# Attention and a token/channel mixer on one core: scores of whole 128-key chunks, barred squares cleared after the exponential, and a new written-out order

## The chip, the cores and the metric

One Trainium2 chip, one core. The time is the device time of one execution in microseconds (us); a lower one is better. Most executions of one kernel agree within 0.3%.

## The reference

Block-wise causal attention (blocks of 64 positions, 8 batches, 8 heads, 576 positions, head size 64), and behind it a mixer over positions and over channels:

```python
scores = scale * np.matmul(q, k.transpose(0, 1, 3, 2))        # q, k, v: (8, 8, 576, 64)
mask = block_i >= block_j                                     # block of a position: pos // 64
scores = np.where(mask, scores, -1000000000.0)
attn = np.exp(scores - max);  attn = attn / (sum + 1e-09)
x = (attn @ v) as (8, 576, 512)
h = np.maximum(xt @ w_tok1, 0.0) @ w_tok2                     # xt: x with positions last
u = x + h.transpose(0, 2, 1)
return u + np.maximum(u @ w_ch1, 0.0) @ w_ch2                 # 512 -> 1536 -> 512
```

Within a 128-key chunk that covers the blocks 2J (keys 0 to 63) and 2J+1 (keys 64 to 127), the queries of block 2J may see the first 64 keys and not the last 64. These 64x64 places are the barred squares.

## The kernel before

**A plan.** The kernel does not emit instructions as it computes. Each helper adds operations to a plan (`P.add`): a piece of work of one or several instructions, with the engines that may run it, what it depends on, and the PSUM banks that it takes and gives back. Operations are numbered as they are added. The string `ORDER` then lists the numbers in the order in which they are emitted; the letter behind a number is the engine (T TensorE, A ScalarE, D DVE, P POOL, S SyncE), and small letters name the PSUM banks taken: a to d are `mm`, e to h are `late`, s and t are two pairs of banks that batch 0's scores use. When the last exponential of batch 0 is done, s and t become e to h. Each engine runs its operations in the order of the list and waits where an operand is not there. Loads are issued from POOL's queue, outputs and large transposes from SyncE's.

**Attention.** Each batch has two groups of four heads (`hg`). `load_qk` brings k and q (L419, L437), DVE transposes them into `kT` and `qT` (L442): a head's 64 dimensions lie as two halves (`par` 0 and 1) in 32 partitions, and four heads fill the 128. `score_set` (L569) computes the scores of a group in three sets, `SETS`, each of one bank of 512 columns per head: set 1 (keys of blocks 2 and 3, and a piece of 0), set 2 (blocks 0 and 1), set 0 (blocks 4 to 8). A tuple of `SETS` is (half, key block, first query block, first column, columns, par). `half` says which 64 partitions of the bank the scores go to, so a matmul holds 64 keys as weights, and the two halves of a 128-key chunk are two matmuls. Where a square is barred, a matmul with `bar` (-2.5e8 times 1.0, key block `None`) opens the place, and the exponential makes it zero.

ScalarE writes the exponentials into `e_sb` (L776; for batch 0 L587 and L737, 1024 columns at a time). `ECOL` and `TAIL` say where a chunk's columns lie. `tail` copies the square at `TAIL` for all heads aside (L595) and then clears its last 64 keys (L600), on DVE or POOL. `head_out` multiplies the exponentials, as weights, with the values `v1` (L617) and divides by the sum; `ends_out` does so for the last 64 positions (L670). `load_v` brings the values (L471).

**The mixer.** `token_mix` (L811, L815, L846, L910) and the channel products follow batch by batch; some of these are done in seven products instead of eight (`channel_up_half` L1111, `channel_up_fast` L1235, `channel_down_fast` L1369), whose sums DVE makes and whose banks ScalarE and DVE empty. The outputs leave at L1421 and L1435.

**The start.** `raise_clock` runs 11 matmuls of 512 columns on zeros (L366), and then up to `KEEP` more (L373), which `ORDER` puts between the first operations; those not listed are not emitted.

Of the kernel before, what the change touches and what calls it, by code (L numbers as in the profile page):

```python
# [10 lines left out]
BF16 = mybir.dt.bfloat16  # L11
# [16 lines left out]
class Plan:  # L28
# [69 lines left out]
    16S 0A 11D 10D 13S 9D 21P 1D 2D 43Ta 5D 19P 4D 3D 23P 33P 27P 14A 25P 31P 15D 29P 17A 20D 37P 44Tb 45Tb 46Tb 22D  # L98
    47Ta 36P 48Ta 49Ta 18D 50Ta 51Ta 52Ta 35P 53Ta 24D 54Ta 55Ta 56Ta 125Ts 34P 100Ttbc 179P 126A 28D 57Ta 58Ta 59Ta
    176P 60Ta 61Ta 26D 62Ta 101A 12P 106Ts 63Ta 32D 182P 64Ta 107A 65Ta 104Tt 42P 30D 66Ta 67Ta 105A 68Ta 39P 123Ts  # L100
    102D 103D 69Ta 70Ta 41P 119A 71Ta 157Tt 124A 112Td 40P 113T 116Ta 108Tb 114D 120A 38P 109T 115D 138Ts 158A 181D
    81P 72Td 73Tc 74Tc 121D 75Tc 122D 139A 82P 76Tc 7D 144Tt 110D 111D 84P 135Td 178D 127Tc 145A 161Ts 185P 136D
    117D 137D 140D 131Tb 180D 83P 128T 162A 142Tt 177D 90P 132T 129D 143A 77Td 89P 163Ts 130D 133D 86P 134D 78Td
    164A 118D 141D 159D 200Tdcba 160D 85P 203A 173Te 154Tf 165Tg 202A 91P 174D 166T 155D 156D 201A 184D 92P 205Tbhfc
    204A 183D 169Td 88P 170T 209A 167D 263Ta 168D 208A 175D 150Tc 171D 261Tg 172D 207A 187D 267Td 206A 87P 186D
    146Te 262A 147T 264A 151T 268D 237Tgbfh 152D 339P 6D 148D 269Ta 153D 241A 149D 273Td 189P 240A 270D 281Tc 239A
    274D 265Te 190P 238A 271Ta 8D 282D 275Tb 266A 191P 193Tdhfg 276A 272D 283Te 196A 277Tc 342P 194A 315Ta 278D
    306Tb 197A 188P 294Td 195A 279Tc 284A 192P 318Tf 198D 280D 291Tg 319T 348P 316T 309Tc 317A 310T 257D 93P 320A
    307T 295T 94P 308A 292T 311A 258D 225Teahf 345P 296A 300Tb 227A 95P 285Tc 228A 286T 293D 226A 303Td 287D 229A
    304T 351P 232Tahge 341D 199D 312Tc 230D 233A 305D 313T 234A 231D 288Tf 344D 314A 297Ta 340D 236A 289T 343D 235A  # L110
    210Td 513P 245Tc 290A 211D 213Th 516P 212D 242Te 246D 216Tg 354P 247D 301T 214D 215D 248Td 243D 302A 298T 244D
    355P 217D 219Tc 249D 299A 250D 222Th 220D 254Te 221D 363Tdbaf 255D 256D 251Tc 349D 364A 330Te 352P 252D 365A
    218D 253D 321Td 367A 223D 224D 366A 259D 353P 368Tcghb 420Ta 372A 370A 422Tb 347D 371A 525P 346D 322T 421D 423A
    260D 369A 356Tafgh 323T 359A 357A 350D 424Tb 360A 324D 331T 358A 425D 388Tcadg 361P 514D 430Tb 391A 434Th 332T
    389A 431D 435A 518D 426Td 392A 517D 400Thcbf 390A 515D 428Tg 404A 393P 362D 334Ta 522P 403A 429D 677P 401A 335T
    333D 402A 528P 427D 376Tb 373Tc 394D 527P 96D 395Tdfgh 379Te 526P 377D 396A 374D 336T 375D 397A 519P 378D 380D
    405Tc 398A 680P 381D 382Tb 399A 406D 385Td 407D 432Te 337D 417Tc 383D 386D 433A 530Tafgh 387D 384D 418D 436Td
    419D 531A 440Tb 97D 414Tc 534A 325Te 533A 98D 326T 532A 415D 437A 416D 542Tahgf 99D 441A 438Tc 545A 327T 439D
    544A 444D 463Tgd 543A 445D 448Thb 328D 466A 464Tc 451D 546A 329S 411Ta 408Te 465A 446D 469T 412D 690P 413D 449Tf
    523D 470A 454T 529P 450A 409D 442Ta 410D 452Tc 455A 443D 691P 467Tg 520D 453A 537Taefh 447D 692P 468A 456T 521D  # L120
    538A 473T 689P 524D 539A 471T 679D 540A 683P 596Ta 457D 541A 474D 562Tcefh 597A 678D 458T 566A 681D 594Ta 565A
    459D 564A 460D 476T 563A 595D 461T 477A 569Tchfe 682D 462A 472D 604Ta 847P 571A 478Tdb 475D 686P 572A 605D 602Tg
    535P 481A 600Th 603D 536P 570A 598Ta 567P 482Tf 601D 607S 568P 553Tc 844P 599D 483A 479Tg 550Th 554D 555D 480A
    488T 551D 484T 552D 606S 489D 486T 485A 556Tc 487D 491T 573A 574Thadg 557D 490D 492A 547Te 558D 577A 493D 497Tbf
    575A 548D 576A 549D 559Tc 578A 688D 701Tedah 498A 685D 579Tg 560D 704A 684D 499T 705A 494D 850P 702A 693P 580D
    585Ta 703A 581D 503T 500D 687D 706Tgdbh 586D 587D 561D 591Te 504D 710A 501Ta 709A 495D 708A 592D 707A 593D 582Tc
    502D 627Tbd 612The 608D 630A 588Tg 583D 496D 505T 859P 615D 858P 633T 584D 506D 507T 857P 634A 589D 590D 860P
    694Tcgab 508D 856P 618T 698A 849D 509T 697A 846D 696A 619D 695A 760Tb 609D 610D 699P 510D 738Tacgh 761A 848D
# [42 lines left out]
    1457D 1392D 1492The 1453D 1393T 1488D 1493A 1489D 1455D 1498T 1394D 1458T 1396S 1460T 1490D 1459D 1472Tca 1468D  # L171
    1465S 1461D 1494T 1464S 1473A 1469D 1476Td 1470D 1478T 1491D 1462T 1479D 1471D 1499D 1482T 1463D 1496Tg 1477D
    1466S 1483D 1502T 1467S 1497D 1484T 1503D 1500T 1507S 1485D 1495D 1480T 1487S 1501D 1474T 1506S 1481D 1504T
    1475D 1486S 1505D 1508S
"""


@with_exitstack
def kernel(
# [340 lines left out]

    BARRED = 2.5e8

# [1057 lines left out]
```

## Time and profile before

| | |
|---|---|
| time, median of 3 runs | 284.84 us (284.22, 284.84, 285.99) |
| profiled execution, first to last instruction | 284.7 us |
| instructions | 9438, of which 4038 matmuls and as many weight loads |
| busy: TensorE matmul / weight load | 275.8 us (97%) / 197.6 us (69%) |
| busy: DVE / ScalarE / POOL | 240.3 (84%) / 180.4 (63%) / 71.7 (25%) |
| granted TensorE clock | full in every slice |
| DMA | 31.79 MB, 112 GB/s in the mean |

How to read it: "busy" is the time in which an engine ran at least one instruction, and an average over stages with different limits. PE is TensorE's matmuls, PEld its weight loads. In a group's row stand line, engine, operation, output<-inputs, shape and count, then busy us, the mean ns of one, and the idle time ahead of it with what ended it. The chain of work that ended last is followed back from the last instruction. "issue" there is time in which the engine waited for nothing that the profile shows. A matmul's record ends later than its last column enters; the distance of starts tells the pace. The span of the profiled execution is what the sums of the prediction are made against; no separate time of that execution was taken.

### The profile page before, as it was taken

How to read it: one execution, taken by the hardware profiler on the slowest of the kernel's cores; microseconds unless marked ns; L12 is line 12 of the kernel's file. 1: busy time of each engine (PE TensorE's matmuls, PEld its weight loads, DVE VectorE, ACT ScalarE, POOL GpSimd, SP SyncE). 2: the span in 40 equal slices, each digit the busy share in tenths (PEclk: the TensorE clock that was granted, in tenths of full speed). 3: DMA queues.
4: the chain of work that ended last, by engine and by line, in shares of the span. 5: the costliest groups of instructions: out<-in, count | busy, mean ns of one | idle time of the engine just before them, and what ended most of it. 6: DMA issues, size and time to landing. Idle time of an engine off the chain costs nothing.

```text
span 284.7 us, 9438 instructions
## 1 busy us (share of the span) xinstructions
PE 275.8 (97%) x4038; PEld 197.6 (69%) x4038; DVE 240.3 (84%) x519; ACT 180.4 (63%) x325; POOL 71.7 (25%) x120
## 2 busy tenths in 40 slices
PE   7998999999999899999999999999999999999994
PEld 3667656556878676987777658744488876468883
DVE  3589569799999799999998997997998987598893
ACT  3798685778888358996879785136546653764000
POOL 8975635170641062060341220000000000000000
PEclk9999999999999999999999999999999999999999
DMA  8999999969989495898199587130033403000246
GB/s 160 166 174 202 190 205 203 137 94 134 144 120 119 71 84 87 225 135 122 11 169 102 87 106 132 49 119 18 2 74 98 126 7 131 12 2 0 104 127 212
DMA packets 64776, 31.79 MB, mean 112 GB/s; under 512 B 53088, under 2 KB 55904, under 8 KB 64736
## 3 DMA queue, kind: packets, MB, share of 16 engines
q0 software_dynamic: 45040, 17.64, 53.1%
q1 hardware_dynamic: 19696, 13.57, 19.6%
q8 instruction: 31, 0.51, 0.7%
q14 instruction: 9, 0.07, 0.1%
HBM read 35.85 MB, written 9.44 MB: 159 GB/s over the span
## 4 chain that ended last, share of the span: by engine, by line
PE 92%; DVE 2%; ACT 2%; DMA 1%; issue 1%; SPq 0%; DVEq 0%
PE late L1369 14%; PE mm L1369 11%; PE late L1235 7%; PE mm L1111 7%; PE late L1111 6%; PE mm L569 6%; PE mm L1235 6%; PE mm L617 4%; PE mm L811 3%; PE mm L910 3%; PE mm L1038 3%; PE late L569 2%; PE late L617 2%; PE late L811 2%; PE mm L1460 2%; PE late L1460 2%
## 5 line engine op out<-in xcount | busy, mean ns | idle before, releaser
L776 ACT ACTIVATE e_sb<-late 128x512 bf16<-128x512 f32 x89 | 50.5, 609 | 10.4 <-PE late L569 9.1
L776 ACT ACTIVATE e_sb<-mm 128x512 bf16<-128x512 f32 x79 | 45.1, 609 | 9.9 <-PE late L569 6.6
L471 POOL DMA_DIRECT2D vals<-in_v_dram x45 | 37.2, 844 | 26.7 <-PE late L617 15.9
L442 DVE STREAM_TRANSPOSE qk_sb<-qk_sb 128x288 int32<-128x288 int32 (+2 forms) x57 | 36.2, 694 | 4.6 <-ACT qk_sb L395 3.5
L1369 PEld LDWEIGHTS <-sums 128*128 128x128 bf16 x288 | 27.6, 98 | 5.6 <-issue 1.8
L1369 PEld LDWEIGHTS <-gT 128*128 128x128 bf16 x288 | 27.8, 98 | 4.6
L569 PEld LDWEIGHTS <-qk_sb 32*64 32x64 bf16 x1280 | 19.9, 104 | 13.1 <-issue 8.8
L569 PE MATMUL mm<-qk_sb 32*64 32x64 bf16 (+7 forms) x546 | 27.8, 291 | 0.0
L569 PE MATMUL late<-qk_sb 32*64 32x512 bf16 (+7 forms) x594 | 27.1, 291 | 0.0
L617 PEld LDWEIGHTS <-e_sb 128*128 128x128 bf16 x640 | 23.8, 97 | 4.1 <-issue 0.9
L1111 PEld LDWEIGHTS <-ws_sb 128*128 128x128 bf16 x192 | 17.8, 98 | 3.4 <-issue 1.3
L797 ACT ACTIVATE gT<-mm 128x512 bf16<-128x512 f32 x25 | 14.7, 601 | 7.8 <-PE mm L1111 3.0
L617 PE MATMUL mm<-vals,e_sb 128*128 128x65 bf16 x430 | 19.0, 193 | 0.0
L643 DVE TENSOR_TENSOR x_sb<-mm,rinv 128x256 bf16<-128x256 f32 x43 | 17.9, 421 | 1.1
L1111 PEld LDWEIGHTS <-wc_sb 128*128 128x128 bf16 x144 | 15.4, 114 | 1.8 <-issue 0.2
L1235 PEld LDWEIGHTS <-ws_sb 128*128 128x128 bf16 x96 | 9.3, 98 | 10.1 <-issue 0.2
L1369 PE MATMUL late<-wd_sb,sums 128*128 128x256 bf16 x108 | 13.6, 272 | 1.2 <-issue 1.2
L1369 PE MATMUL late<-wd_sb,gT 128*128 128x256 bf16 x120 | 14.7, 273 | 0.0
L595 POOL COPY vals<-e_sb 128x256 bf16<-128x256 bf16 x10 | 4.1, 412 | 40.9 <-issue 22.9
L395 ACT COPY mm<-late 128x512 f32<-128x512 f32 x17 | 9.9, 584 | 7.1 <-PE late L1235 5.0
L797 ACT ACTIVATE gT<-late 128x512 bf16<-128x512 f32 x17 | 10.2, 602 | 6.3 <-PE late L1235 3.4
L1235 PE MATMUL late<-e_sb,ws_sb 128*128 128x512 bf16 x44 | 12.6, 379 | 0.0
(203 smaller groups left out, 656.2 us busy)
## 6 DMA issues: line engine op xcount, KB each, us to landing
out_dram<-o_sb SPq DMA_DIRECT2D x14, 512.0 KB, 3.1
vals<-in_v_dram POOLq DMA_DIRECT2D x28, 128.0 KB, 5.4
qk_sb<-in_k_dram POOLq DMA_DIRECT2D x12, 288.0 KB, 6.3
qk_sb<-in_q_dram POOLq DMA_DIRECT2D x12, 288.0 KB, 5.9
out_dram<-o_sb SPq DMA_DIRECT2D x7, 256.0 KB, 3.2
wc_sb<-in_moe_w_ch_dram POOLq DMA_DIRECT2D x8, 192.0 KB, 7.7
wc_sb<-in_moe_w_ch_dram POOLq DMA_DIRECT2D x3, 512.0 KB, 10.4
vals<-in_v_dram POOLq DMA_DIRECT2D x15, 64.0 KB, 4.9
```

The source lines that it names most:

```text
L442: nc.vector.transpose(dst[:, 0:S, :] .rearrange("p s e -> p (s e)") .bitcast(I32) .rearrange("p (a k) -> p k a", k=NB)[:, k0:k1], raw2.bit ...
L471: nc.gpsimd.dma_start(out=t[128 - p : 128, J, hs, 0:64], in_=src)
L569: nc.tensor.matmul(out=home(n)[64 * half : 64 * half + 64, c : c + w], lhsT=bar[r, 0] if j is None else kT[i][r, 64 * j : 64 * j + 64, par ...
L617: nc.tensor.matmul(out=u[:, I, 0:65], lhsT=e[:, h, c : c + 128], rhs=vt[:, J, head, 0:65], start=(J == 0), stop=(J == I),)
L643: nc.vector.tensor_tensor(out=xt[:, 0:4, 64 * head : 64 * head + 64], in0=u[:, :, 0:64], in1=ri[:, 0:4].to_broadcast([128, 4, 64]), op=MULT,)
L776: nc.scalar.activation(dst, bank_of(x), EXP, scale=scale)
L797: nc.scalar.activation(dst, src, RELU)
L811: nc.tensor.matmul(out=ps, lhsT=w1_sb[:, c, tt : tt + 255 : 2], rhs=xt[:, c, cols], start=(c == 0), stop=False)
L1111: nc.tensor.matmul(out=bank_of(bank)[:, 256 * o_ : 256 * o_ + 256], lhsT=x(o_, m), rhs=y[:, :, m, :], start=opens, stop=m == 1, skip_group ...
L1235: nc.tensor.matmul(out=bank_of(bank), lhsT=x(m), rhs=y[:, :, m, :], start=first and m == 0, stop=m == 1, skip_group_check=not first,)
L1369: nc.tensor.matmul(out=bank_of(bank)[:, 256 * i : 256 * i + 256], lhsT=x[:, kk, 128 * i : 128 * i + 128], rhs=y[:, kk], start=first and i ...
L1460: nc.tensor.matmul(out=ps, lhsT=gT[0][:, cc, 128 * si : 128 * si + 128], rhs=wc2_sb[:, cc, :], start=cc == 0, stop=cc == NDC - 1,)
```

## The change

1. The second and third score sets no longer work on halves: `half` is `None`, the weights are 128 keys wide (32 rows by 128 columns of the array for a head), and the output covers all 128 partitions. The first set keeps halves; its columns are laid out anew so that both halves of the chunk of blocks 4 and 5 start at the same query.
2. The tile `bar`, its two memsets and its matmuls go. The barred squares are computed like the others, and `clear` writes zeros over them in `e_sb` after the exponentials: two squares of 64 columns per head in each call, one call behind the first set (where `tail` cleared one square) and a new one behind the second set. A head's output waits for the clears of its group, and so for all exponentials of the second set.
3. 29 of the up to 37 warming matmuls are listed instead of 35; three of four have 512 columns instead of 256.
4. `ORDER` is another list altogether. Because operations are numbered as they are added, the same work has another number in it (before minus 2, plus the new clears added ahead of it).

```diff
-                    out=bank_of(bank)[:, 0:256], lhsT=zeros[:, 0:128], rhs=zeros[:, 0:256],
-                    start=True, stop=True,
+            w = 512 if n % 4 else 256
...
+                    out=bank_of(bank)[:, 0:w], lhsT=zeros[:, 0:128], rhs=zeros[:, 0:w], start=True, stop=True,
...
     SETS = (
         (
-            (0, 4, 4, 0, 320, 0), (1, None, 0, 0, 64, 0), (1, 5, 5, 64, 256, 0),
-            (0, 4, 4, 0, 320, 1), (1, 5, 5, 64, 256, 1),
-            (0, 6, 6, 320, 192, 0), (1, 8, 8, 320, 64, 0), (1, 7, 7, 384, 128, 0),
-            (0, 6, 6, 320, 192, 1), (1, 8, 8, 320, 64, 1), (1, 7, 7, 384, 128, 1),
+            (0, 4, 4, 192, 320, 0), (1, 5, 4, 192, 320, 0), (0, 4, 4, 192, 320, 1), (1, 5, 4, 192, 320, 1),
+            (0, 6, 6, 0, 192, 0), (1, 8, 8, 0, 64, 0), (1, 7, 7, 64, 128, 0),
+            (0, 6, 6, 0, 192, 1), (1, 8, 8, 0, 64, 1), (1, 7, 7, 64, 128, 1),
         ),
         (
-            (0, 2, 2, 0, 448, 0), (1, None, 0, 0, 64, 0), (1, 3, 3, 64, 384, 0),
-            (0, 2, 2, 0, 448, 1), (1, 3, 3, 64, 384, 1),
-            (0, 0, 0, 448, 64, 0), (1, None, 0, 448, 64, 0), (0, 0, 0, 448, 64, 1),
+            (None, 2, 2, 0, 448, 0), (None, 2, 2, 0, 448, 1), (None, 0, 0, 448, 64, 0), (None, 0, 0, 448, 64, 1),
         ),
         (
-            (0, 0, 1, 0, 512, 0), (1, 1, 1, 0, 512, 0), (0, 0, 1, 0, 512, 1), (1, 1, 1, 0, 512, 1),
+            (None, 0, 1, 0, 512, 0), (None, 0, 1, 0, 512, 1),
         ),
     )
-    ECOL = (448, 0, 1024, 1344)
-    TAIL = 1344
+    ECOL = (448, 0, 1216, 1024)
+    TAIL = 1024
+    BARRED = ((1024, 192), (0, 448))
...
+                rows, keys = (slice(0, 128), 128) if half is None else (slice(64 * half, 64 * half + 64), 64)
...
-                        out=home(n)[64 * half : 64 * half + 64, c : c + w],
-                        lhsT=bar[r, 0] if j is None else kT[i][r, 64 * j : 64 * j + 64, par],
-                        rhs=bar[r, 1] if j is None else qT[i][r, 64 * q : 64 * q + w, par],
+                        out=home(n)[rows, c : c + w],
+                        lhsT=kT[i][r, 64 * j : 64 * j + keys, par],
+                        rhs=qT[i][r, 64 * q : 64 * q + w, par],
...
+        return copied, clear(0, hg, hs, [copied], prio, urgent)
+
+    def clear(n, hg, hs, deps, prio, urgent=0):
+        c0, step = BARRED[n]
+        late_keys = e_sb[hg][64:128, hs, c0 : c0 + 2 * step].rearrange("p h (a c) -> p h a c", a=2)[:, :, :, 0:64]
+
+        def emit(o):
+            (nc.vector if o.engine == "DVE" else nc.gpsimd).memset(late_keys, 0.0)
...
+                elif s == 1:
+                    these = [clear(1, hg, slice(0, 4), these, prio + 0.1)] * 4
```

Places of the new list that the prediction speaks of. At the start of batch 1 (`202T` is its first score set, `208T` the next; 51, 74, 61 and 50 are warming matmuls):

```
129D 130D 184P 134D 51Th 39P 74Th
208Thabd 210A 164D 186D 37P 161P 175Tf 171Tc 172T 61Tg 267Tg 185D 176D 173D 174D 209A 187P 155Tc 177D 167Tf 188D
189D 50Ta 268A
```

On POOL between batches 5 and 6 (916 and 980 are clears, 1057, 1060 k and q of batch 7, 1064 and 1065 values of batch 7, 964 values of batch 6):

```
829T 830D 911Thdea 961D 885A 913A 895Tb 896D 959D 889Tf 897D 915A 890D 891D 914A 912A 831D 832T 833A 916P 892Td
893D 894D 937Ta 938A 898Tf 899D 900D 901Tb 934Tg 981Tdahe 902D 903D 922Tf 935D 936D 923D 924D 983A 931Tb 932D
933D 928Tg 984A 985A 958D 673Ta 1057P 968Tbfeh 982A 801A 925Td 1064P 1065P 970A 972A 971A 929D 674D 962D 1060P
969A 930D 926D 927D 677T 676D 678D 1008Tghfd 1010A 1012A 1011A 939Te 964P 816D 940A 834D 975Thabd 976A 979A
1053D 977A 978A 980P 1052D 973D 974P 679T 1014Thefd 1017A 1018A 943Ta 1009A 1013P 680D 681T 944D 1056D 682D
1015A 1001Tadfb 1062D 1003A 1016A 683S 992Th 993D 1055D 989Tc 995Tg 996D 1067P 1005A 684S 990D 994D 991D 1063P
```

and the end of the list, before and after:

```
before: 1506S 1481D 1504T 1475D 1486S 1505D 1508S
after:  1520T 1521D 1503A 1496T 1497D 1524S 1502S
```

More of the change, by code (lines that the diff above doesn't have):

```diff
@@ L103 @@
[L103 to L107, printed above, removed]
@@ L342, in fill @@
                 pads.setdefault(key, []).append(P.add(engine, 0.17 if engine == "DVE" else 0.32, emit, (), prio))
-        fill("DVE", "bar", -1e5 + 1, (bar[:, 0, :], -BARRED), (bar[:, 1, :], 1.0))
         for i in range(2):
@@ L578, in score_set @@
         op = P.add(
-            "PE", 0.48, emit, deps + pads["bar"], prio, take=notes, mode=1, urgent=2 * (b == 0),
+            "PE", 0.48, emit, deps, prio, take=notes, mode=1, urgent=2 * (b == 0),
         )
@@ L597, in tail @@
         copied = P.add(TAILS, {"DVE": 0.15, "POOL": 0.4}, emit_copy, deps + list(et_war), prio, urgent=urgent)
[L599 to L603 removed]
+        return copied, clear(0, hg, hs, [copied], prio, urgent)
[4 more added lines that the diff above has]
+            (nc.vector if o.engine == "DVE" else nc.gpsimd).memset(late_keys, 0.0)
+        return P.add(
+            TAILS, {"DVE": 0.17 if urgent else 0.24, "POOL": 0.5}, emit, deps, prio, urgent=urgent
         )
@@ L751, in first_attention @@
                     these = [cleared]
+                elif n == 1:
+                    these = [clear(1, hg, hs, these, prio + 0.1, urgent=1)]
                 exps += these
```

152 lines of the change are left out of this document (72 added, 80 removed).

## The prediction

> **What bounds the kernel now.** I read the busy line and the slices first, then a table by stage, then the chain that ended last, in order of time.
>
> ```profile
> PE 275.8 (97%) x4038; PEld 197.6 (69%) x4038; DVE 240.3 (84%) x519; ACT 180.4 (63%) x325; POOL 71.7 (25%) x120
> PEclk9999999999999999999999999999999999999999
> PE 92%; DVE 2%; ACT 2%; DMA 1%; issue 1%; SPq 0%; DVEq 0%
> ```
>
> ```profile
> 8.30:20.80 12.50, 12.31 (x298) 8.12 (x297) 8.52 (x29) 11.63 (x14) 10.64 (x19) 1.00 1.49 172
> 20.80:58.00 37.20, 36.44 (x674) 23.03 (x674) 28.80 (x72) 28.11 (x56) 17.23 (x26) 1.00 1.34 182
> 58.00:180.00 122.00, 120.44 (x2319) 91.04 (x2312) 113.25 (x267) 93.21 (x179) 36.61 (x60) 1.00 0.88 114
> 180.00:280.50 100.50, 100.50 (x734) 72.48 (x731) 85.75 (x141) 44.69 (x74) 0.00 (x0) 1.00 0.24 69
> 280.50:284.70 4.20, 0.04 (x1) 0.00 (x0) 0.42 (x1) 0.00 (x0) 0.00 (x0) 1.00 0.49 180
> ```
>
> ```profile
> 19.75 1.01 ACT e_sb L587
> ...
> 20.81 0.51 PE late L670 x20
> ...
> 27.68 0.75 issue
> ...
> 93.13 1.24 issue
> ...
> 278.57 1.31 PE mm L1369 x12
> ...
> 280.57 0.42 DVE o_sb L1393
> ```
>
> The reader is to see three stages. Up to 20.8 us the end is set by ScalarE's exponentials of batch 0 (11.63 of 12.50 us busy); TensorE fills that time with warming matmuls. From 20.81 to 280.5 us TensorE itself is the chain: it idles 0.76 us to 58 us, 1.56 us to 180 us, and not at all behind that. The last 4.2 us are one DVE add and the output transfer. So three things can move the time: the columns that TensorE streams between 20.8 and 280.5 us, its idle time there (2.3 us in all), and the two ends. All work of the other engines counts only where TensorE comes to wait for it. The granted clock is full in every slice.
>
> **The score sets.** The change halves the instructions of the second and third set, and leaves the first nearly as it was. Per group of four heads it takes 44+32+16 = 92 matmuls down to 40+16+8 = 64; over 16 groups 448 of 4038 go. What a set takes now:
>
> ```profile
> 105.23 0.27 PE L815 MATMUL mm<-x_sb,w1o_sb 128*128 128x256 bf16 x1
> 105.43 0.41 PE L569 MATMUL mm<-qk_sb 32*64 32x512 bf16 x2
> ...
> 105.71 0.39 PE L569 MATMUL late<-qk_sb 32*64 32x512 bf16 x2
> 106.02 0.28 PE L1111 MATMUL mm<-th_sb,ws_sb 128*128 128x256 bf16 x1
> ```
>
> ```profile
> 16.01 0.64 PE L569 MATMUL sc<-qk_sb 32*64 32x512 bf16 x8
> ...
> 16.58 0.32 PE L670 MATMUL mm<-vals,e_sb 128*64 128x65 bf16 x8
> ```
>
> ```profile
> 104.26 1.03 PE L811 MATMUL mm<-x_sb,w_sb 128*128 128x512 bf16 x4
> ...
> 108.52 0.33 PE L569 MATMUL mm<-qk_sb 32*64 32x320 bf16 x3
> ...
> 109.14 0.32 PE L670 MATMUL late<-vals,e_sb 128*64 128x65 bf16 x8
> ...
> 111.72 0.39 PE L569 MATMUL late<-qk_sb 32*64 32x448 bf16 x1
> ...
> 112.30 0.61 PE L910 MATMUL late<-aT,w_sb 128*128 128x512 bf16 x2
> ```
>
> ```profile
> 32.27 1.29 PE late L1038 x6
> ```
>
> A 512-column matmul streams in 1.29/6 = 0.215 us. The third set streams two rounds, 0.43 us, and occupies 106.02-105.43 = 0.59 us, because the second round starts 0.26 us after the first and the next group 0.10 us after the last column; another 0.09 us pass ahead of it (105.23 plus 0.11 for 256 columns, to 105.43). The instructions themselves are cheap: eight matmuls start within 0.02 us. The nearest row for half as many instructions is the set of two heads: 8 matmuls instead of 16, the same two rounds, 0.57 us. Columns per head stay 1024 in every set, 64 or 128 keys wide. So I take 0.015 us off each third set and as much off each second (0.58 us now): 28 sets behind 20.8 us, -0.4 us. The first set (0.62 us) I leave; batch 0's sets lie under ScalarE. Bounds: below, nothing of the gap between rounds is left (two rounds of 0.215 and 0.10 behind them, 0.53 us), 0.05 less for 28 sets, -1.4 us. Above, the weights for 128 columns are no longer loaded under the first round:
>
> ```profile
> L569 PEld LDWEIGHTS <-qk_sb x1280: 101/103/111, 8.0 to 172.2; 32*64 32x64 bf16 x183
> ```
>
> ```profile
> 105.43 0.16 PEld L569 LDWEIGHTS <-qk_sb 32*64 32x64 bf16 x16 [0.21 <-issue]
> ```
>
> ```profile
> L373 PEld LDWEIGHTS <-wd_sb x35: 95/98/142, 5.9 to 19.6; 128*128 128x128 bf16 x35
> ```
>
> All 16 loads of a set now begin in its first 0.16 us, and 64 columns take 103 ns, 128 columns 98 ns. If a load came to stand bare at both rounds, 28 x 2 x 0.10 = +5.6 us. I stay near the low end: the 128-column row is no longer than the 64-column one.
>
> A rule speaks against this. The Trainium skill, "TensorE: Matmul & The Clock Gate", section "LDWEIGHTS (loading the stationary operand)", has a load take its columns over 1.2 per ns, so that 128 columns cost 107 ns and 64 cost 53. By that, an estimate, each of the 28 sets would begin 0.05 us later, +1.5 us instead of -0.4. The two rows above do not show that dependence, and I go by the rows.
>
> **Order on TensorE.** Going into and out of a group of another array shape costs those 0.09 and 0.10 us. Counting neighbours in the two lists, the array changes its shape 122 times before and 118 times after (sets of 64 and of 128 columns counted as different): -0.4 us.
>
> **Warming.** 35 of 256 columns become 19 of 512 and 10 of 256. Their place matters. Before, the last stands ahead of the first score set of batch 1, under the exponentials. After, that set takes three `late` banks (`202Tcefg`), which are given out only by the last exponential of batch 0 (20.76 us above), and four warming matmuls stand behind it: `51Th`, `74Th`, `61Tg`, `50Ta`, two of each width.
>
> ```profile
> 15.36 0.72 PE L373 MATMUL mm<-wd_sb 128*128 128x256 bf16 x5
> ```
>
> Five of 256 columns take 0.72 us with the 0.27 us of the last one's record, 0.11 us each; so 2 x 0.215 + 2 x 0.11 = +0.65 us where TensorE is already the chain. If the values or the DVE are late there, they fill idle time and cost nothing; bounds 0 to +0.65. I take +0.6. The clock gains nothing: it is full already.
>
> **Two waits on "issue".** At 27.68 and 93.13 us TensorE stands in the middle of a group whose operands were there, and the trace names no releaser.
>
> ```profile
> q8 instruction: 31, 0.51, 0.7%
> ```
>
> I read them as late instructions, which arrive in 31 packets of 16 KB; that is an inference. With 8076 loads and matmuls down by 2 x 454 the packets fall on other places. Both may go (-2.0 us), stay (0) or come more often (+1). I take half, -1.0.
>
> **Cleared squares.** Removed: two memsets of `bar`. Added: 18 clears for the second set, and a clear twice as wide for the first. After, 6 of the 18 run on DVE, 12 on POOL.
>
> ```profile
> L600 POOL MEMSET e_sb<- 64x256 bf16 x9 | 2.8, 306 | 5.6 <-PE mm L910 5.2
> L595 POOL COPY vals<-e_sb 128x256 bf16<-128x256 bf16 x10 | 4.1, 412 | 40.9 <-issue 22.9 <-ACT e_sb L776 17.9
> L471 POOL DMA_DIRECT2D vals<-in_v_dram x45 | 37.2, 844 | 26.7 <-PE late L617 15.9 <-PE mm L617 4.5 <-PE mm L815 1.9
> ```
>
> ```profile
> L340 DVE MEMSET wd_sb<- x1: 272/272/272, 1.3 to 1.3; 128x256 uint32 x1
> ```
>
> ```profile
> vals<-in_v_dram POOLq DMA_DIRECT2D x28, 128.0 KB, 5.4
> ```
>
> ```profile
> DMA to landing us min/median/max: 3.4/5.2/11.8
> ```
>
> POOL pays about 0.5 us for each, some 7 us more on an engine that is 25% busy; DVE at most 18 x 0.27 = 5 us on 240. The work hides under TensorE. What can show is POOL's queue, which is strictly in order: a clear waits for four exponentials, and loads stand behind it. The tightest place is `1064P 1065P 1060P 964P`: two value loads of batch 7 wait for batch 5's last head output (`925T`), and a value load of batch 6 stands behind them. From there to its reader (`992T`) TensorE has three products of 1.31 us, a token product of 1.08 (104.26 to the last column at 105.34), one of 0.43 (two of 512 columns) and four sets of about 0.7: 8.2 us. The load needs 0.2 + 2 x 0.88 + 0.55 us to be issued and 5.4 us to land, 7.9. Slack 0.3 us where before the least such lead was 11.9 us; the landings of these loads spread from 3.4 to 11.8 us, and one of 6.8 makes it +1.1. I take +0.3. Were the cover gone at every group, a clear on POOL and the wait behind it cost 0.5 us x 14, +7 us, far from any row.
>
> **The end.** The last transfer becomes `1502S`, a row of 512 columns (256 KB), for `1508S`, a piece of 128 KB.
>
> ```profile
> out_dram<-o_sb SPq DMA_DIRECT2D x7, 256.0 KB, 3.2
> ...
> out_dram<-o_sb SPq DMA_DIRECT2D x2, 128.0 KB, 2.6
> ```
>
> That is +0.6 us; but the bytes behind the last add are shared with the transfer ahead of it, so 0 to +0.6, I take +0.3. One transfer there goes to ScalarE's queue, which is idle.
>
> **Sum**, against the span of 284.7: -0.4 sets, -0.4 shapes, +0.6 warming, -1.0 issue, +0.3 queue, +0.3 end = -0.2, so 284.5. The median of the three runs, 284.84, stands 0.14 above that span; as a median of runs I expect 284.6.
>
> **Rivals.** (1) *TensorE sheds its gaps.* Both issue waits vanish (-2.0) and the rounds close up (-1.4): -2.0 -1.4 -0.4 +0.6 = -3.2, 281.6. For it: those waits have no operand behind them, and 11% of the instructions go. Against: no row has a set under 0.57 us. Chance 0.17. (2) *Bare weight loads*, the slower side: between the two rounds of a 128-column set the four row strips are all in use, so loads wait for them. Price 28 x 0.2 = 5.6 us, and the 0.4 us are not saved: 290.6; over 1% it decides from 0.10 us a set. Against it stands the row with 16 loads in 0.16 us. The Trainium skill, "TensorE: Matmul & The Clock Gate", section "The mechanism" under packing small matmuls, lets a load overlap running matmuls only on other row strips; the trace's loads for the second round, on strips in use, disagree. Chance 0.12. (3) *POOL's queue holds loads.* The lead of 8.2 us turns into a wait at batch 6, and the stage up to 58 us, where the DMA share of the table is still 1.34, brings others: 2 or 3 waits of 1.1 to 1.5 us, +3.0, 287.6. For: 29 waiting clears and copies on POOL where 19 were. Against: no such wait in before. Chance 0.19. That the edits cancel, each hidden or small, is my forecast, 0.52.
>
> **Numbers.** A measurement here tells about 1% from no change: 282.0 and 287.7. Forecast's own range 282.8 to 286.6. Faster: 0.13 of rival 1 and 0.03 of the forecast's tail, 0.16. Slower: 0.11 of rival 2, 0.10 of rival 3, 0.04 of the tail, 0.25. Same: 0.59. The range takes rival 1 whole and rival 3, and leaves most of rival 2 out: 281.5 to 289.0.
>
> **What would show it.** Right: 3584 or so matmuls; second and third sets at 0.56 to 0.58 us; 118 shape changes; PE busy from 21 to 280 us with idle under 3 us; DVE busy up by 2 to 5 us and unseen; the last transfer 256 KB. Wrong: sets at or over 0.65 us or under 0.55; PE waiting for `vals` ahead of L617 at batch 6; new waits on `e_sb` L600; PE starting its unbroken run later than 22 us.

## The result, and the profile after

The changed kernel takes **295.56 us** (median of four runs, 293.30 to 296.58) beside 284.53 us for the kernel before on the same chip: a ratio of 1.0376, 95% interval [1.0324, 1.0427]. It is slower by 11 us, 10.7 above the median that the prediction started from, and lies outside its range of 281.5 to 289.0. Ratios here leave out runs that the comparison counts as disturbed.

The page of the changed kernel; the execution shown spans 291.5 us (before: 284.7), and its time was 293.30 us:

```profile
PE 278.3 (95%) x3584; PEld 194.4 (67%) x3584; DVE 246.6 (85%) x533; ACT 172.9 (59%) x317; POOL 78.7 (27%) x130
PEclk9999999999999999999999899999999999999999
q8 instruction: 28, 0.46, 0.6%
PE 77%; DMA 10%; POOL 5%; DVE 4%; issue 3%; SPq 0%; ACT 0%; DVEq 0%; POOLq 0%
PE mm L1372 12%; PE late L1372 8%; PE late L1238 7%; PE mm L1238 5%; PE mm L1114 5%; PE late L1114 5%; DMA vals<-in_v_dram 5%; PE late L616 4%; PE late L562 4%; DMA uT<-u_sb 3%; PE mm L562 3%; PE mm L1463 3%; PE mm L1041 3%; PE late L913 3%; PE mm L616 2%
```

454 matmuls are gone, as intended. But TensorE was 92% of the chain that ended last and is now 77%; 10% of the chain is transfers, which were 1%. Two are named: value loads and the transposes of `uT`. One slice of the clock, the 23rd, is not full.

The table by stage, with the bounds used before as far as they fit (stretch and its length, then busy us and instructions of PE, PEld, DVE, ACT, POOL, granted clock, DMA share, GB/s):

```profile
8.30:20.80 12.50, 11.07 (x209) 6.35 (x203) 8.62 (x29) 11.35 (x14) 10.94 (x20) 1.00 1.40 173
20.80:58.00 37.20, 35.95 (x594) 22.46 (x594) 30.47 (x81) 28.06 (x57) 18.11 (x29) 1.00 1.33 187
58.00:180.00 122.00, 117.05 (x1934) 84.94 (x1933) 109.74 (x256) 92.68 (x178) 42.38 (x67) 0.99 0.85 109
180.00:280.50 100.50, 100.50 (x767) 72.54 (x766) 88.98 (x150) 37.63 (x66) 0.00 (x0) 1.00 0.21 61
280.50:291.50 11.00, 6.62 (x58) 5.37 (x56) 5.10 (x13) 0.00 (x0) 0.00 (x0) 1.00 0.62 184
```

From 58 to 180 us TensorE idles 4.95 us where it idled 1.56; from 20.8 to 58 us 1.25 instead of 0.76; and a new idle time of about 1 us lies behind 280.5 us. What it waited for, from the list of waits (waiting engine and line, releaser: us in total, times, longest):

```profile
PE late L616 <- DMA vals<-in_v_dram: 3.0, 1, 3.0
PE late L1114 <- DVE th_sb L1086: 1.6, 1, 1.6
PE mm L616 <- DMA vals<-in_v_dram: 1.3, 1, 1.3
PE late L1372 <- DVE o_sb L1396: 0.9, 1, 0.9
PE late L849 <- issue: 0.8, 1, 0.8
PE late L562 <- issue: 0.3, 1, 0.3
```

The 1.3 us lie in batch 0, under ScalarE's exponentials: batch 1's first set still starts at 20.88 us, where TensorE became the chain at 20.81 before. The others lie on the path. The largest stands at 156 us (TensorE's timeline, then POOL's, then pieces of the chain):

```profile
156.32 0.23 PE L616 MATMUL late<-vals,e_sb 128*128 128x65 bf16 x2
159.58 0.60 PE L616 MATMUL late<-vals,e_sb 128*128 128x65 bf16 x8 [3.03 <-DMA vals<-in_v_dram]
...
161.09 1.73 PE L814 MATMUL mm<-x_sb,w_sb 128*128 128x512 bf16 x4
```

```profile
148.48 1.78 POOL L469 DMA_DIRECT2D vals<-in_v_dram  x2 [0.47 <-PE mm L616]
150.24 0.57 POOL L417 DMA_DIRECT2D qk_sb<-in_q_dram  x1
150.79 0.91 POOL L469 DMA_DIRECT2D vals<-in_v_dram  x1
```

```profile
115.70 9.51 DMA uT<-u_sb
...
150.79 8.76 DMA vals<-in_v_dram
```

Two value loads and a query load of batch 7 stand on POOL until batch 5's last head output at 148.48 us; the load of batch 6 behind them is issued at 150.79 and lands 8.76 us later, while its reader has been ready since 156.4. Just behind, four 512-column matmuls take 1.73 us instead of the usual 1.02: the clock.

```profile
156.40:159.50 3.10, 0.16 (x2) 0.06 (x3) 0.84 (x2) 2.56 (x5) 1.80 (x3) 0.94 1.49 290
159.60:162.30 2.70, 2.70 (x31) 1.93 (x31) 1.77 (x7) 0.00 (x0) 1.34 (x2) 0.50 1.35 105
```

For 2.7 us behind the wait the granted clock is 0.50. The wait at 124 us is of another kind: a product waits for DVE's `th_sb`, and that for a transpose of `uT` which was issued at 115.70 us and took 9.51 us.

The distances between TensorE's starts give the balance. From batch 1's sets at 20.8 us to the start of the last matmul pass 266.9 us after and 259.5 before, +7.4. TensorE's idle time in that stretch, added up from the tables, is 1.25 + 4.95 + 0.9 = 7.1 us where it was 2.3: +4.8. The half clock adds about 1.4 us (2.7 us of work at half speed in the row above, so 1.35 us more than at full speed); the rest, about 1.2 us, is spread over small distances. The tail behind the last matmul is 0.7 us shorter. That makes 6.7 of the 6.8 us between the two spans.

The two profiled executions are not the middle ones of their kernels. That of the changed kernel is the shortest of its four; the other three span 294.7, 292.8 and 294.7 us at mean clocks of 0.983, 0.988 and 0.983, where the profiled one had 0.994. A clock of 0.983 is 0.017 x 292 = 5 us of TensorE's time, so these runs lose more to the clock than the profile shows. The kernel before, timed again beside the experiments, spans 281.9 to 284.6 us, 282.8 in the median, and its times lie 1.7 to 1.8 us above its spans. The 284.7 us of its profile are thus longer than any of these, and stand for a time of about 286.4 us. The 11 us between the medians are therefore more than the 6.8 us between the profiles.

### The profile page after: what moved, and what is told of

It reads as the page before. It is cut to its first block, busy times and chain, and to the rows that moved or that the text cites. A ratio compares the mean times of both kernels' runs of the same rounds, so it can differ in the third digit from the quotient of the medians.

```text
span 291.5 us, 8548 instructions
## 1 busy us (share of the span) xinstructions
PE 278.3 (95%) x3584; PEld 194.4 (67%) x3584; DVE 246.6 (85%) x533; ACT 172.9 (59%) x317; POOL 78.7 (27%) x130
## 4 chain that ended last, share of the span: by engine, by line
PE 77%; DMA 10%; POOL 5%; DVE 4%; issue 3%; SPq 0%; ACT 0%; DVEq 0%; POOLq 0%
PE mm L1372 12%; PE late L1372 8%; PE late L1238 7%; PE mm L1238 5%; PE mm L1114 5%; PE late L1114 5%; DMA vals<-in_v_dram 5%; PE late L616 4%; PE late L562 4%; DMA uT<-u_sb 3%; PE mm L562 3%; PE mm L1463 3%; PE mm L1041 3%; PE late L913 3%; PE mm L616 2%
## 5 line engine op out<-in xcount | busy, mean ns | idle before, releaser
L469 POOL DMA_DIRECT2D vals<-in_v_dram x45 | 37.2, 833 | 16.2 <-PE late L616 10.7
L562 PE MATMUL mm<-qk_sb 32*64 32x320 bf16 (+6 forms) x480 | 28.1, 272 | 0.2 <-DVE rinv L636 0.2
L562 PE MATMUL late<-qk_sb 32*64 32x320 bf16 (+6 forms) x436 | 27.2, 277 | 0.3 <-issue 0.3
L562 PEld LDWEIGHTS <-qk_sb 32*64 32x64 bf16 (+1 forms) x1024 | 17.0, 99 | 15.3 <-issue 9.8
L393 ACT COPY mm<-late 128x512 f32<-128x512 f32 (+1 forms) x16 | 9.3, 579 | 21.4 <-PE late L1372 13.2
L616 PE MATMUL late<-vals,e_sb 128*128 128x65 bf16 x370 | 17.4, 196 | 3.0 <-DMA vals<-in_v_dram 3.0
L599 POOL MEMSET e_sb<- 64x512 bf16 (+1 forms) x23 | 12.0, 528 | 20.0 <-ACT e_sb L777 15.1
L642 DVE TENSOR_TENSOR x_sb<-late,rinv 128x256 bf16<-128x256 f32 x37 | 15.2, 416 | 0.7
L393 ACT COPY late<-mm 128x512 f32<-128x512 f32 (+1 forms) x15 | 8.4, 563 | 11.7 <-PE mm L1372 4.2
L1396 DVE TENSOR_TENSOR o_sb<-mm,u_sb 128x512 f32<-128x512 f32 x17 | 11.7, 688 | 4.0 <-PE mm L1372 2.8
L417 POOL DMA_DIRECT2D qk_sb<-in_k_dram x12 | 6.6, 549 | 28.0 <-DVE qk_sb L440 21.7
```

The costliest lines, as they stand in the source:

```text
L393: nc.scalar.copy(dst, src)
L469: nc.gpsimd.dma_start(out=t[128 - p : 128, J, hs, 0:64], in_=src)
L562: nc.tensor.matmul(out=home(n)[rows, c : c + w], lhsT=kT[i][r, 64 * j : 64 * j + keys, par], rhs=qT[i][r, 64 * q : 64 * q + w, par], start ...
L599: (nc.vector if o.engine == "DVE" else nc.gpsimd).memset(late_keys, 0.0)
L616: nc.tensor.matmul(out=u[:, I, 0:65], lhsT=e[:, h, c : c + 128], rhs=vt[:, J, head, 0:65], start=(J == 0), stop=(J == I),)
L642: nc.vector.tensor_tensor(out=xt[:, 0:4, 64 * head : 64 * head + 64], in0=u[:, :, 0:64], in1=ri[:, 0:4].to_broadcast([128, 4, 64]), op=MULT,)
```

## The experiments

Theory at the start: **the loss lies in the new order**, which leaves some transfers no lead; the tiles gain what the trace shows, and the clears hide. Rivals: the tiles cost; the clears cost, on POOL's queue or as a link.

**1. One load moved.**

```diff
- ... 1065P 1060P 964P 816D ...      (964P behind the loads of batch 7)
+ ... 824A 965P 964P 827T ...        (beside its sister load)
```

> The changed kernel with one value load of batch 6 (964) moved from behind the loads of batch 7 to behind its sister load 965, where its buffer has long been free. Theory (transfers that the new order issues late): the wait of 3.19 us at 156 us goes, and with it the token product at half speed behind it, 0.7 us; nothing else is touched, so 295.6 falls to about 291.7. Rival (the load is only the first of many that come late; the next takes its place): under 1 us, 294.6 or more. Rival (the profiled wait is not on the path): no change.

290.07 us (289.48 to 293.18), ratio to before 1.0212 [1.0154, 1.0270]: -5.5 us. The reader now starts on time:

```profile
157.40 0.21 PE L562 MATMUL mm<-qk_sb 32*64 32x128 bf16 x1
157.55 0.47 PE L616 MATMUL late<-vals,e_sb 128*128 128x65 bf16 x10
157.86 0.46 PE L616 MATMUL mm<-vals,e_sb 128*128 128x65 bf16 x10
158.16 0.46 PE L616 MATMUL late<-vals,e_sb 128*128 128x65 bf16 x10
158.47 1.02 PE L814 MATMUL mm<-x_sb,w_sb 128*128 128x512 bf16 x4
```

The wait is gone and the token product is back at 1.02 us. The gain is larger than the 3.9 us expected; three of the four runs now have a clock of 0.999 or 1.0, and none had in the changed kernel.

**2. The same load late in the kernel before**, the reverse.

```diff
- ... 768A 951P ...                  (load of batch 6, before)
+ ... 1052P 951P ...                 (behind a load of batch 7)
```

> The kernel before with one thing of the change: a value load of batch 6 (number 951 there) stands behind a value load of batch 7 that waits for batch 5's last head output. Theory: it is issued at about 148.7 us, lands 5.5 us later at 154.2, and its reader at about 151.9 waits 2 to 3 us, with up to 1 us of half clock behind it: 287.0 to 288.5. Rival (the wait is filled or the load lands in 3.4 us): 285. Rival (one long wait lowers the clock for longer): 289 or more, at a granted clock of 0.99 or less.

287.23 us, ratio 1.0113 [1.0065, 1.0160]: +2.7 us, inside the expected range.

```profile
150.41 0.39 PE L568 MATMUL late<-qk_sb 32*64 32x512 bf16 x2
152.45 0.46 PE L616 MATMUL late<-vals,e_sb 128*128 128x65 bf16 x10 [1.65 <-DMA vals<-in_v_dram]
```

One step of the change, done alone, brings the wait at this place. It is 1.65 us long, shorter than the 2 to 3 us expected. The rest of the 2.7 us is not shown to come from the load: in this execution batch 0 waits 1.4 us on a transpose by DVE (0.5 us in the profile before) and TensorE becomes the chain at 21.66 us instead of 20.81. The load was second of four in the queue here and landed in 5.2 us. The clock stayed at 0.997 or above in three of four runs and fell to 0.994 in the slowest (289.65 us).

**3. The tiles alone**, in the order of before.

```diff
-            (0, 0, 1, 0, 512, 0), (1, 1, 1, 0, 512, 0), (0, 0, 1, 0, 512, 1), (1, 1, 1, 0, 512, 1),
+            (None, 0, 1, 0, 512, 0), (None, 0, 1, 0, 512, 1),
     (the second set likewise, its bars dropped)
```

> The kernel before, its order kept, with the second and third set in tiles of 128 keys; the second set's barred squares are left unbarred, neither by matmul nor by a clear (batch 0 as well). Theory (wide tiles are cheaper, order and clears cost): 42 sets at 0.015 to 0.027 us less, 283.6 to 284.2 beside 284.7. Rival (weight loads of 128 columns stand bare): 287 or more. Rival (the second order kernel, 293.4, lost its time to the tiles): 290 or more; if it is 284, that one lost it to the clears where they were put in.

284.07 us, ratio 0.9979 [0.9962, 0.9996]: -0.5 us, and the profile has no wait of TensorE over 0.3 us behind the start. The gain, of the wide tiles together with the bars left out, is small and its interval ends just under 1; the rival of bare weight loads falls. The Trainium skill, "TensorE: Matmul & The Clock Gate", section "LDWEIGHTS (loading the stationary operand)", would have 128 columns take twice as long to load as 64. The changed kernel's row, which holds both, shows one narrow range instead:

```profile
L562 PEld LDWEIGHTS <-qk_sb x1024: 91/103/109, 7.3 to 174.5; 32*64 32x64 bf16 x104, 32*128 32x128 bf16 x67
```

**4. The order and warming alone**: the tiles, bars and narrow clears of before in the order of after.

```diff
     ORDER = (that of the changed kernel, less its 18 clears)
     SETS, bar, clears: those of the kernel before
```

> The kernel before, its 64-key tiles, its bars by matmul and its narrow clears kept, in the order of the changed kernel and with its warming matmuls; the 18 clears drop out of the order. Theory (the loss lies in the order): 294 to 297, the score sets cost 0.8 us more than in the changed kernel and the waits at 124 and 156 us are there. Rival (the wider tiles with their clears cost it): 286 or less. Rival (order and clears only together): in between, 288 to 291.

297.83 us, ratio 1.0417 [1.0343, 1.0492]. The order, with its warming matmuls, brings the whole loss without the tiles and the clears. The waits, in an execution of 298.99 us, the longest of the four:

```profile
PE late L616 <- issue: 3.3, 1, 3.3
PE late L616 <- DMA vals<-in_v_dram: 2.4, 1, 2.4
PE late L568 <- issue: 2.2, 2, 1.9
PE mm L616 <- DMA vals<-in_v_dram: 1.5, 1, 1.5
```

The late load of batch 6 is there (2.4 us). The wait at 124 us that I expected is not: its place is taken by 3.3 us on "issue", to which I come below. So the same order loses by another mix here: the waits on "issue" are longer than those on transfers. The other three executions were not traced.

**5. The changed kernel without the second set's clears** from batch 1 on.

```diff
-                elif s == 1:
-                    these = [clear(1, hg, slice(0, 4), these, prio + 0.1)] * 4
```

> The changed kernel, its order kept, without the 14 clears of the second set from batch 1 on (the barred squares of that set are left unzeroed). Theory (late transfers by their place in the order): the waits at 123.8 and 156.4 us stay, 294.5 to 296.5; the loads stand behind the head outputs of batch 5, not behind a clear. Rival (the clears, 0.5 us each on POOL's queue with the wait for four exponentials, hold the loads): 291 or less, and no wait for vals at batch 6.

294.52 us in the median of all four (290.97 to 300.72); the ratio, 1.0255 [1.0206, 1.0304], is that of the two shortest, 290.97 and 292.85. The times alone do not decide: the median meets the theory's range, the shortest the rival's. The wait stays, here in the execution of 296.18 us:

```profile
PE late L615 <- DMA vals<-in_v_dram: 2.9, 1, 2.9
PE mm L615 <- DMA vals<-in_v_dram: 1.5, 1, 1.5
PE late L1111 <- DVE th_sb L1083: 1.4, 1, 1.4
```

So the clears do not hold the load; its place behind batch 7's loads does. The four spans follow the clock: 289.1 us at 1.0, 291.0 at 0.994, 294.3 at 0.977, 298.8 at 0.966. At 0.994 the changed kernel spans 291.5, so by this one pair the 14 clears cost about 0.5 us. Stretches of the one at 0.977:

```profile
13.00:16.00 3.00, 1.50 (x53) 1.18 (x52) 0.36 (x2) 2.84 (x4) 1.90 (x4) 1.00 1.49 193
16.50:26.00 9.50, 9.50 (x98) 4.77 (x97) 6.78 (x23) 4.75 (x6) 6.42 (x13) 0.50 1.30 178
```

Behind the 1.5 us wait in batch 0, which cost nothing by itself, TensorE ran 9.5 us at half clock. The same wait (1.3 us) left the clock at 1.00 in the profile of the changed kernel.

**6. The changed tiles and clears in the order of before.**

```diff
     ORDER = (that of the kernel before, renumbered, warming 256 wide, and 18 clears on DVE:)
+ ... 403A 688P 386D 387Tb 404A 405D 411Tc ...     (405D: a clear; 411Tc: its head output)
```

> The changed tiles and clears in the order of the kernel before, its warming matmuls of 256 columns too; the 18 clears are put in on DVE, each behind the exponentials it needs, and three head outputs stand one or two places later for that. Theory (the loss lies in the order): the sets give 0.8 us, some of it lost to the clears, so 283.5 to 285.0 beside 284.5 for the kernel before. Rival (wider tiles or the clears cost it): 290 or more. Rival (the clears as an added link between exponential and head output cost 0.3 us at each of 16 groups): 287 to 289.

293.35 us, ratio 1.0318 [1.0277, 1.0359]. My theory missed by 9 us: the tiles are innocent (experiment 3), so what remains are the clears as I had placed them, and the three head outputs moved for them.

```profile
PEld L616 <- DVE e_sb L599: 4.4, 4, 1.6
DVE e_sb L599 <- ACT e_sb L777: 3.1, 9, 0.7
PE mm L616 <- DVE e_sb L599: 2.3, 3, 1.2
PE late L616 <- DVE e_sb L599: 1.1, 1, 1.1
```

Head outputs wait for clears, 3.4 us in all by TensorE's two rows, and DVE stands at clears until the exponentials come, with evacuations behind it. That these evacuations make up the rest of the 9 us is argued, not shown. This left open whether a clear costs by itself, or only without lead.

**7. Nine clears with lead**, in the order of before: the third set wide everywhere, the second wide only in the nine groups with 8 us between last exponential and first head output, their clears on POOL.

```diff
+    CLEARED = ((1, 0), (2, 0), (3, 0), (3, 1), (4, 0), (5, 0), (6, 1), (7, 0), (7, 1))
...
+            for half, j, q, c, w, par in WIDE if s == 1 and (b, hg) in CLEARED else SETS[s]:
```

> The order of the kernel before, the third set in wide tiles everywhere, the second set in wide tiles with a clear only in the nine groups of four heads where the order leaves 8 us or more between the last exponential and the first head output; those clears stand on POOL, where the exponentials have long been done. The other groups keep their bars; the whole result is computed. Theory (a clear costs nothing where it has lead; the second order kernel lost 9 us because its clears had none): no wait on a clear, and 284.0 to 284.8, with 1 us more if an instruction packet comes late. Rival (the clears cost by themselves, on POOL's queue or as a link): 286.5 or more.

> The same with every second warming matmul split in two (some 17 more matmuls and as many loads ahead of everything). Theory: the same work, so it differs from the kernel without the split only where an instruction packet comes late; both between 283.7 and 285.7, the lower of them at 284.2. Rival (the clears cost by themselves): both at 286.5 or more.

286.62 us (1.0075 [1.0047, 1.0102]) and 285.81 us (1.0044 [1.0028, 1.0060]). Neither profile has a wait on a clear. The waits of the first:

```profile
PE mm L619 <- issue: 1.2, 1, 1.2
PE late L672 <- issue: 1.0, 1, 1.0
PE late L672 <- ACT e_sb L589: 0.3, 1, 0.3
```

With 8 us of lead no product waits for a clear. In time the theory missed: it had both at 285.7 or less, and both intervals lie above 1. The first fell on the rival's bound, the second, with the same clears, below it. The traces put 2.2 us of the first and 1.4 us of the second on "issue"; that the clears cost nothing else is not shown by the times.

**8. The third set alone, and two shifts.** First the third set wide and all else as before; then every or every second warming matmul split into two of 128 columns, which only moves the instructions behind it.

```diff
+                w = 128 if n % 2 else 256          (every second; "n < 99" for all)
+                for c in range(0, 256, w):
+                    nc.tensor.matmul(out=bank_of(bank)[:, c : c + w], ...)
```

> The kernel before with the third set alone in tiles of 128 keys; bars, clears, order and warming as before, the whole result computed. Theory: 14 sets behind 20.8 us at 0.027 us less, -0.4, 284.3. Rival (no gain to be had: the rounds are bound by streaming): 284.7. Rival (fewer instructions move the instruction packets and a wait of 1 us comes or goes): 283.3 or 285.7.

> The kernel with the third set alone in wide tiles (285.9, one wait of 1.0 us on issue at 63.7 us, 0.5 us behind the landing of an instruction packet), each of its 35 warming matmuls split into two of 128 columns: the same columns under batch 0's exponentials, 70 more instructions on TensorE ahead of everything that follows. Theory (issue waits are late instruction packets, and where packet ends fall in the program decides): the wait at 63.7 us goes or moves; without another in its place 284.0 to 284.4, with one 285 to 286. Rival (the wait belongs to that score set, whatever the packets): 285.9 and a wait in the same set.

> The same with every second warming matmul split, some 34 more instructions. Theory as for the shift by 70, with packet ends elsewhere again: a wait on issue stands only 1.3 to 1.6 us ahead of work that follows an instruction packet's landing, at another place than 63.7 us; time 284.0 to 286.0. Rival (place of the packets does not matter): 285.9 and the same wait. Rival (the warming matmuls themselves cost): over 286.

285.91 us (1.0040 [1.0022, 1.0059]) for the third set alone; 285.43 (1.0025 [1.0009, 1.0042]) with all split; 284.50 (0.9997 [0.9983, 1.0012]) with half of them split. The same work differs by 1.4 us in the median. The kernel without splits, in the middle of a score set (timeline, TensorE):

```profile
63.67 0.25 PE L570 MATMUL late<-qk_sb 32*64 32x192 bf16 x3
64.68 0.22 PE L570 MATMUL late<-qk_sb 32*64 32x64 bf16 x2 [0.76 <-issue]
```

In the other two this wait is gone, so it belongs to the place of the instructions and not to the score set. It does not account for the 1.4 us, though: the traced execution took 284.62 us, the shortest of its twelve, and the traced one with half split 284.56. What the longer executions waited for was not traced. The one with all split stands 0.9 us above the one with half. Its profile has 1.2 us on DVE's transposes at 6.8 us, in batch 0, but its last matmul starts only 0.3 us later (278.3 and 278.0 us); another 1.05 us of the 1.3 us between the two spans lie behind that. Its clock of 0.995 comes from half speed behind 280.9 us, where TensorE has no work left, and cost nothing. What the waits on "issue" have in common is an instruction packet that lands shortly before TensorE goes on. From the records of queue q8 (us):

```
kernel                     packet lands   TensorE goes on   later by
before                            26.93             28.43       1.50
before                            92.98             94.37       1.39
after                             30.18             31.58       1.40
order of after                    33.53             35.06       1.53
order of after                   127.63            129.05       1.42
third set alone                   63.23             64.68       1.45
nine clears                       44.04             45.52       1.48
nine clears                       66.20             67.51       1.31
```

The traces of all kernels hold 20 waits of TensorE on "issue" of 0.25 us or more, and it always goes on 1.3 to 1.6 us after such a landing. The packets also follow TensorE's instructions in number: 31 for 8076 matmuls and weight loads before, 28 for 7168 after. I read these waits as late instructions; where they fall depends on how many instructions stand ahead.

**9. More lead for the other late transfers.** A first attempt moved two value loads:

```diff
- ... 762Tg 966P 963P ...
+ ... 870P 966P 963P ...             (and 964P as in experiment 1)
```

> The changed kernel with load 964 early as in the first run, and the two value loads 966 and 963 of batch 6, which it issues at 115.7 us, moved behind load 870 of batch 5, some 5 us later. Theory (the transposes of uT issued at 113 and 115.7 us are late because they share the queues with these loads): the wait of 1.8 us at 124 us goes or falls under 0.6, 288.5 beside 290.1 of the first run. Rival (such transposes take 9 to 10 us beside any load; the place of two loads does not matter): 290, wait unchanged. Rival (the two loads become late in their turn): 291 or more.

292.53 us (289.00 to 293.31), ratio 1.0247 [1.0193, 1.0302]; the wait at 124 us stayed at 1.4 us. The aim was off: the loads that the trace shows at 113 to 116 us are 868, 951, 954, 869 and 867; 966 and 963 come later. It says nothing on the theory. At a full clock this run spans 287.2 us (profiled), so the larger median is the clock: 0.994, 0.988 and 0.982 in the other three.

The second attempt moved the right ones, and two folds at the end (additions by DVE of a product into the output):

```diff
- ... 733D ... 951P 747P 954P ...    + ... 960P 951P 954P ...
- ... 1490T 1491D ... 1511D ...      + ... 1479D 1511D 1491D ...
```

> The changed kernel with three late transfers given more lead: value load 964 as in the first run; the loads 951 and 954 of batch 6's keys and queries (issued at 114 and 115 us, beside the transposes of uT) behind load 960, some 7 us later; and at the end the folds 1511 and 1491 behind 1479, so that DVE does not stand at an output transfer. Theory (what is left of the loss is transfers without lead, not tiles or clears): the waits of 1.6 to 1.8 us at 124 us and 0.8 to 1.0 us at 280 us go; at full clock the span falls from 288.2 (first run) to about 285.7, 287.4 us of time. Rival (the next late thing takes their place): 289 or more at full clock. Rival (the transposes are slow by themselves): 288.5, the wait at 124 us unchanged.

288.24 us (286.74 to 290.46), ratio 1.0137 [1.0096, 1.0179]. At full clock the span is 284.9 us: 6.6 less than the changed kernel's profiled run, of which about 1.4 was half clock. The product of `th_sb` no longer waits:

```profile
122.83 0.60 PE L1114 MATMUL late<-uT,wc_sb 128*128 128x256 bf16 x4
123.27 0.60 PE L1114 MATMUL late<-th_sb,ws_sb 128*128 128x256 bf16 x4
123.70 0.47 PE L616 MATMUL late<-vals,e_sb 128*128 128x65 bf16 x10
```

The transposes were late because of the loads beside them: the longest now takes 7.2 us instead of 9.5. The step at the end did not work: the wait for `o_sb` moved from 284 to 276 us and still takes 0.8 us. With 0.8 us on "issue" at 30 us and 0.6 us for an ends' output (L669) at 156 us, this is 2.2 of the 2.9 us that still separate this span from that of the tiles alone (282.0). In time, experiments 1 and 9 together bring the ratio from 1.0376 to 1.0137, some 7 of the 11 us; the last 4 us were not taken apart.

## Why the prediction was wrong, by its steps

**What bounds the kernel**: right. TensorE's idle time behind 20.8 us makes most of the loss; the 1.3 us ahead of it, in batch 0, do not show.

**The sum itself**: its six terms add up to -0.6, not to -0.2, so they gave 284.1 us and not 284.5. And the 0.14 us between span and median were no such distance: times lie 1.7 to 1.8 us above spans, and the execution that I started from was longer than any timed later. Neither explains the miss.

**Score sets, -0.4**: right in direction, under-sized. From a set's start to the next group's, in the median, the third takes 0.563 us (0.590 before), the second 0.567 (0.582), the first 0.600 (0.616): 0.8 us over 14 of each. Second and third alone, without their bars, gave 0.5 us of time (experiment 3). Bare weight loads, the second rival, did not come.

**Array shapes, -0.4**: this term should have been nothing. The 118 changes are as counted, but they take in batch 0, which lies under ScalarE. Behind 20.8 us the matmuls of the two traces change their shape 97 times before and 99 times after. What one change is worth was not separated by any run.

**Warming, +0.6**: right. TensorE's timeline behind 20.88 us:

```profile
21.45 0.50 PE L372 MATMUL late<-wd_sb 128*128 128x512 bf16 x2
21.88 0.40 PE L562 MATMUL late<-qk_sb 32*128 32x512 bf16 x1
...
23.25 0.38 PE L372 MATMUL late<-wd_sb 128*128 128x512 bf16 x1
23.46 0.33 PE L814 MATMUL late<-x_sb,w_sb 128*128 128x128 bf16 x3
```

0.43 and 0.21 us pass there with no other work; the pair at 21.45 is one of 512 and one of 256 columns, and the last one, of 256, takes 0.11 us at 24.50.

**Waits on "issue", -1.0**: the reading as late instructions held. In the two profiles they went from 1.9 to 1.1 us, so the number is near; but it is luck, as the 3.3 us in experiment 4 and their coming and going in experiment 8 show. Nor is it known whether the middle executions of the kernel before have these waits at all. The bounds I gave, -2.0 to +1, were too narrow on the slow side.

**POOL's queue, +0.3**: this step failed. The place was right and so was the lead: from 148.48 to 156.4 us are 7.9 us where I had 8.2. The queue took 2.3 us ahead of the load, 2.5 in the sum. What was mis-sized is the landing: 8.76 us, where I took the median of all such loads, 5.4, and 6.8 as the bad case, with 11.8 in the quoted row. This load was issued fourth of four within 3.2 us, and SyncE issued two output transfers of 512 KB each from 150.87 us on, which moved their data from 154 to 160 us. The load moved in experiment 2, second of four and with no output beside it, landed in 5.2 us. Which of the two made it slow was not separated; either way it was not a median one. The cost was a wait of 3.0 us, and about 1.4 us of half clock, for which no step had a term: 4.4 us where the sum had 0.3. In the runs it was 5.5 us (experiment 1). This is the place that the third rival named, to which I gave 0.19; but it had two or three waits of 1.1 to 1.5 us where one of 3.0 us came, and the clears that spoke for it were not the cause (experiment 5).

**Transfers not looked at.** I checked the lead of value loads only. The transposes of `uT` (1.6 us) were late because of loads beside them (experiment 9), and the output buffer at the end cost 0.9 us, from a cause that experiment 9 did not settle. No step named either. For an order that is new throughout, the lead of each kind of transfer had to be compared.

**The end, +0.3**: wrong in sign. The last column to the end takes 3.4 us instead of 4.2; the larger last transfer cost nothing, but the wait for `o_sb` ahead of it did.

**Clears**: all but hidden in the new order, as said (about 0.5 us by the one pair of spans in experiment 5). That they were free anywhere would have been wrong (experiment 6).

## What to carry to other kernels

A change that forces a new hand-written order is to be priced by the order: compare, for each kind of transfer, the lead from issue to first reader before and after, and set it against the landing of a load inside its cluster and beside the outputs of that time, not against the median. A wait of TensorE can cost more than its length, since the clock may fall behind it. Differences of about 1 us between kernels with thousands of instructions may be nothing but the place of the instructions in the program (experiment 8); shift them before believing such a difference.

## What the runs showed of the hardware that was not expected

The granted clock falls to 0.50 behind some of TensorE's waits: for 3.4 us with a wait of 3.0 us (changed kernel, from 159.1 us on), for 10.2 us behind 1.5 us (experiment 5, from 16.2 us on), and not at all behind other waits of 1.3 to 1.7 us. The Trainium skill, "TensorE: Matmul & The Clock Gate", section "What's actually happening", tells of two states only and of a free-running window of about 3.4 us. The rows agree on the two states, 0.50 and 1.00, and a free-running window would let the same wait cost the clock in one run and not in the next. The clock records of the traces agree on the window as well: ahead of the last matmul the six stretches at 0.50 are 3.41 us long, or in one case three times that, 10.24 us. They do not agree on the way back: TensorE was busy for all of 9.50 us at 0.50, in this one trace. What in those 9.5 us kept the clock down was not tried.

These steps of 3.41 us also tell much of which wait costs the clock. By these traces it is TensorE's idle time within one step that counts, more than the length of the wait. Over all fifteen traces, a step with 2.28 us or more of it always had half speed behind it, and from a step with 1.49 us or less the clock never fell. In between both occur: it fell behind 1.50 and 1.89 us, and not behind six steps with 1.65 to 1.99 us at the ends of kernels; what decides there is open. The wait of 1.6 us at 124 us in the changed kernel lies across two steps, 0.89 us in one and 0.75 in the next, and the clock stayed full.

A transposing transfer of `uT` took 9.51 us among five loads on POOL's queue, where 3.2 us is the median, and the wait for it went when two of those loads were moved away. In the kernel before the longest one took 10.6 us, and TensorE did not wait for it: there it had the lead. An instruction that comes late lets TensorE go on 1.3 to 1.6 us after its packet has landed.
